# Leaving out two zeroings by GpSimd ahead of the first mixture-of-experts sums

## The chip, the cores and the metric

The kernel runs on one core of a Trainium2 chip. The metric is device time in microseconds (us) for one execution. The engines work side by side, each through its own queue in order: TensorE (PE; PEld are its weight loads), VectorE (DVE), ScalarE (ACT), GpSimd (POOL) and SyncE (SP), whose queue here issues most DMAs.

## The reference

Causal attention with a decay bias on (4, 8, 576, 64), then a top-1 mixture of 8 experts on the 2304 resulting rows of 512, then a feed-forward layer with h·cos(h):

```python
scores = scale * q @ k.T + minimum(-(cum_i - cum_j), 0)      # causal
attn   = softmax(scores);  x = (attn @ v) as (2304, 512)
idx    = argmax(xn @ en.T / tau);  gate = softmax(...)[idx]
for e in range(8):
    h = maximum(x[idx == e] @ w1[e], 0)
    out[idx == e] = gate * (h @ w2[e])
h = out @ w_in;  y = (h * cos(h)) @ w_out                    # 2304 x 512
```

## The kernel before, in words

Three stages follow each other, and their seams overlap. `attention` runs to about 215 us. It routes the rows batch by batch: POOL scatters each batch's rows to `xr` in DRAM, grouped by expert (L431). After the third of four batches one expert is chosen, and the first 256 of its rows are read back early and transposed into `the` and `tle`.

`moe1` is the first stage of sums. It takes nine "rounds": round -1 is the chosen expert on those 256 early rows, round 0 the same expert on its late 128 rows, rounds 1 to 7 the other experts. Each round has 8 steps f, one per slice of 128 hidden units. A step has a first product, `emit_h` (L727 to L729: 4 blocks, each as high·high, high·low and low·high halves, 12 matmuls), a relu that ACT writes as high half `hh` (L732) and DVE completes as low half `hl` (L733), and a second product `emit_o` one step later (L760 to L762: 12 matmuls into four sums `acc`). In TensorE's queue this gives h(n), o(n-1), h(n+1), o(n) and so on. At the end of a round the four sums go to SBUF: ACT writes the high half into `x2h` (L767), DVE the low half into `x2l` (L768), each at a column offset of that expert that is read from a register. `x2h` and `x2l` hold 2304 columns for all experts, and `moe2` reads them for the last two products.

Weights come through a ring of six slots. SP loads a chunk (L660) when a slot is free, ACT casts it to the high half (L662), DVE subtracts for the low half (L664). Round 0 uses full fp32 weights without a split: two chunks fill one slot (L657). SP's queue holds, in order: the eight chunks of round -1, three pairs for round 0, the late rows `xw` (L675), the first rows of round 1, the last pair of round 0, chunks of round 1. A load into a slot waits until the o step that last read it is done.

Beside this, DVE works through small operations of `counts` (L538 to L575), which sort the experts; ACT, DVE and SP read their results as registers (`pki`, L584 and L591).

The two zeroings stand in `moe1` before its loop, behind the last scatter of `attention` on POOL's queue. They set columns 344 to 2303 of `x2h` and `x2l` to zero, 4 x 1960 = 7840 fp32 a partition each. The sums written later cover the columns of the routed rows; a column that no round writes belongs to a row that the tail loop `overflow` computes again. SP's order is fixed by the program; DVE's, ACT's and POOL's order comes from a scheduler.

Of the kernel before, what the change touches and what calls it, by code (L numbers as in the profile page):

```python
# [7 lines left out]
F32 = mybir.dt.float32  # L8
# [10 lines left out]
B, H, S, D = 4, 8, 576, 64  # L19
NT, DM = 2304, 512  # L20
E, F = 8, 1024

EARLY, LATE = 256, 128
# [15 lines left out]
@with_exitstack  # L39
def moe_kernel(ctx, tc, qd, kd, vd, sd, ied, embt, tau, ident, maskd, trid, wcat, wf, out):  # L40
    nc = tc.nc
    const = ctx.enter_context(tc.tile_pool(name="const", bufs=1))
    dram = ctx.enter_context(tc.tile_pool(name="dram", bufs=1, space=DRAM))
    xr = dram.tile([E * NT, DM], F32, name="xr")
    count = ctx.enter_context(tc.tile_pool(name="count", bufs=1))

    g = G()
    g.count = count
    early = ExitStack()
    ep = early.enter_context(tc.tile_pool(name="early", bufs=1, side="right"))  # L50
    g.the = ep.tile([128, 4, EARLY], F32R, name="the")
    g.tle = ep.tile([128, 4, EARLY], F32R, name="tle")
    g.tc, g.nc, g.const, g.dram, g.xr, g.out = tc, nc, const, dram, xr, out
    with tc.manual_schedule(engines={mybir.EngineType.SP, mybir.EngineType.PE}):
        attention(g, qd, kd, vd, sd, ied, embt, tau, ident, maskd, trid)
    with tc.manual_schedule(engines={mybir.EngineType.SP}):
        st = ctx.enter_context(ExitStack())
        g.rawp = st.enter_context(tc.tile_pool(name="rawp", bufs=3, reuse_waits="tile"))
        g.ringp = st.enter_context(tc.tile_pool(name="ringp", bufs=RING, reuse_waits="tile"))
        g.x2p = st.enter_context(tc.tile_pool(name="x2p", bufs=1, reuse_waits="tile"))  # L60
        g.cv = st.enter_context(tc.tile_pool(name="cv", bufs=1, reuse_waits="tile"))
        g.chunks, g.tasks, g.loading = {}, [], {}
        moe1(g, wcat, wf)
        early.close()
        moe2(g, wf)
        st.close()
    with tc.manual_schedule():
        overflow(g, wcat, wf)
# [446 lines left out]
def moe1(g, wcat, wf):  # L515
    tc, nc, const, dram, xr = g.tc, g.nc, g.const, g.dram, g.xr
    SL = NT + CAPS[1]
    x2p = g.x2p
    x2h = x2p.tile([128, 4, SL], F32R, name="x2h")
    x2l = x2p.tile([128, 4, SL], F32R, name="x2l")  # L520
    g.x2h, g.x2l = x2h, x2l
    tid = g.tid = dram.tile([NT, 1], I32, name="tid")
    with ExitStack() as st:
# [118 lines left out]
            nc.vector.tensor_copy(out=g.win, in_=win)  # L642


        steps = [(r, f) for r in range(-1, E) for f in range(8)]
        loads = [(-1, f) for f in range(8)] + [(0, f) for f in range(0, 8, 2)] + [(r, f) for r in range(1, E) for f in range(8)]

# [137 lines left out]
                tc.declare_no_dep(ins.ins, o, reason="rows that differ")  # L785
            prev.append(ins.ins)


        c0 = (B - 1) * S // E + LATE
        with tc.issue_after(g.last.ins):  # L790
            nc.gpsimd.memset(x2h[:, :, c0:NT].bitcast(F32), 0.0)
            nc.gpsimd.memset(x2l[:, :, c0:NT].bitcast(F32), 0.0)
        NS = len(steps)
        for n in range(NS):
            r, f = steps[n]
# [289 lines left out]
```

## Time and profile before

| | |
|---|---|
| median of 3 runs (lowest, highest) | 893.03 us (891.38, 895.02) |
| the profiled execution | 895.34 us, of which the span is 893.5 us |
| mean granted TensorE clock | 0.982 |
| PE busy, DVE, ACT, POOL | 853.0, 612.4, 435.1, 139.2 us |
| `attention` / `moe1` / `moe2`, about | 0 to 215 / 215 to 480 / 480 to 893 us |

The span runs from the first to the last instruction; what lies around it is 1.8 us. Of TensorE's clock, 1.00 stands for 2.4 GHz and 0.50 for 1.2 GHz. In a timeline, an operation's time runs to its end, so operations of one engine that stand in its pipeline together overlap.

### The profile page before, as it was taken

What the parts mean: (1) busy time and instruction counts of PE and PEld (TensorE: products, weight loads), DVE (VectorE), ACT (ScalarE), POOL (GpSimd) and SP (SyncE); (2) the same over time, 40 slices, a digit from 0 to 9 for tenths busy, and PEclk for the clock granted to TensorE, in tenths of its full rate; (3) what the DMA queues carried; (4) which work ended last, traced back from release to release, by engine and by line L of the source; (5) the groups of instructions that cost most, each with busy time, mean ns of one, the idle gap of its engine ahead of it and who ended that gap; (6) DMA issues with size and microseconds to landing.
All of it is one profiled execution on the core that took longest, in us unless ns stands there. A gap on an engine that the chain in (4) does not pass through costs nothing. (4 is left out here: it accounts for less than half of the span.)

```text
span 893.5 us, 14901 instructions
## 1 busy us (share of the span) xinstructions
PE 853.0 (95%) x5286; PEld 691.0 (77%) x5286; DVE 612.4 (69%) x1611; ACT 435.1 (49%) x928; POOL 139.2 (16%) x156
## 2 busy tenths in 40 slices
PE   7999999997499999999999999999999999999994
PEld 3556565656499999999998888888888888888883
DVE  4778878887928555655679977777687748644452
ACT  3876767764325444554545555333343334333331
POOL 3422726340800111111000000000000000000132
PEclk9999999998799999999999999999999999999998
DMA  9999756313485676697654221111021100000112
GB/s 257 257 320 250 244 151 215 105 55 121 145 313 190 147 169 164 134 177 186 168 165 119 72 93 48 48 48 48 14 70 50 47 12 0 1 1 1 47 74 95
DMA packets 41871, 107.69 MB, mean 121 GB/s; under 512 B 9022, under 2 KB 9406, under 8 KB 41790
## 3 DMA queue, kind: packets, MB, share of 16 engines
q1 hardware_dynamic: 38190, 97.14, 38.6%
q0 software_dynamic: 3552, 9.45, 2.8%
q8 instruction: 44, 0.72, 0.3%
q14 instruction: 37, 0.30, 0.1%
q10 hardware_dynamic: 48, 0.07, 0.0%
HBM read 90.83 MB, written 15.81 MB: 119 GB/s over the span
## 5 line engine op out<-in xcount | busy, mean ns | idle before, releaser
L664 DVE TENSOR_TENSOR wl<-wraw,wh 128x1024 fp32r<-128x1024 f32 x64 | 78.4, 1226 | 75.3 <-ACT wh L662 72.5
L985 PE MATMUL h_ps<-x2h,wh 128*128 128x512 f32 (+1 forms) x320 | 118.3, 371 | 0.0
L987 PE MATMUL h_ps<-x2h,wl 128*128 128x512 f32 (+1 forms) x320 | 118.3, 370 | 0.0
L986 PE MATMUL h_ps<-x2l,wh 128*128 128x512 f32 (+1 forms) x320 | 118.1, 369 | 0.0
L1005 PE MATMUL facc<-wh,gh 128*128 128x512 f32 x288 | 114.8, 399 | 1.5 <-ACT gh L992 1.5
L1007 PE MATMUL facc<-wh,gl 128*128 128x512 f32 x288 | 113.9, 396 | 0.0
L1006 PE MATMUL facc<-wl,gh 128*128 128x512 f32 x288 | 113.8, 395 | 0.0
L846 ACT ACTIVATE ki<-h_ps 128x512 int32<-128x512 f32 (+1 forms) x80 | 44.6, 557 | 119.4 <-PE h_ps L987 114.4
L847 DVE SCALAR_TENSOR_TENSOR ki<-ki,h_ps 128x512 f32<-128x512 int32 (+1 forms) x80 | 50.6, 632 | 71.1 <-ACT ki L846 65.3
L662 ACT CAST wh<-wraw 128x1024 fp32r<-128x1024 f32 x64 | 67.0, 1048 | 61.2 <-PE acc L761 45.6
L283 ACT ACTIVATE s_sb<-s_sb,mx 128x576 f32<-128x576 f32 (+2 forms) x144 | 83.7, 583 | 21.1 <-DVE mx L278 17.4
L761 PE MATMUL acc<-hl,wh 128*128 128x256 f32 (+7 forms) x256 | 77.8, 305 | 12.8 <-DVE hl L733 12.8
L1017 POOL DMA_INDIRECT out_dram<-oacc,ti x18 | 17.5, 972 | 434.6 <-DVE oacc L1015 431.0
L848 ACT ACTIVATE ki<-ki,hpi 128x512 f32<-128x512 f32 (+1 forms) x80 | 54.5, 682 | 47.0 <-DVE ki L847 46.3
L762 PE MATMUL acc<-hh,wl 128*128 128x256 f32 (+7 forms) x256 | 77.4, 303 | 0.0
L760 PE MATMUL acc<-hh,wh 128*128 128x256 f32 (+7 forms) x256 | 76.6, 305 | 0.0
L992 ACT CAST gh<-ki 128x512 fp32r<-128x512 f32 (+1 forms) x80 | 46.2, 578 | 51.6 <-DVE ki L849 51.1
L986 PEld LDWEIGHTS h_ps<-x2l,wh 128*128 128x128 f32 x320 | 60.1, 188 | 12.3 <-issue 0.4
L985 PEld LDWEIGHTS h_ps<-x2h,wh 128*128 128x128 f32 x320 | 60.0, 188 | 12.2 <-issue 0.2
L987 PEld LDWEIGHTS h_ps<-x2h,wl 128*128 128x128 f32 x320 | 60.1, 188 | 11.2
L849 DVE TENSOR_TENSOR ki<-h_ps,ki 128x512 f32<-128x512 f32 (+1 forms) x80 | 50.7, 634 | 25.8 <-ACT ki L848 24.2
L727 PE MATMUL h_ps<-xth,wh 128*128 128x368 f32 (+6 forms) x224 | 68.2, 304 | 0.0
(218 smaller groups left out, 1884.4 us busy)
## 6 DMA issues: line engine op xcount, KB each, us to landing
wraw<-in_wcat_dram SPq DMA_DIRECT2D x64, 512.0 KB
wraw<-in_wf_dram SPq DMA_DIRECT2D x32, 512.0 KB
c_t<-cumd SPq DMA_DIRECT2D x15, 576.0 KB
xr<-zr SPq DMA_DIRECT2D x8, 768.0 KB
v_t<-in_vd_dram SPq DMA_DIRECT2D x16, 320.0 KB
q_t<-in_qd_dram SPq DMA_DIRECT2D x16, 288.0 KB
k_t<-in_kd_dram SPq DMA_DIRECT2D x16, 288.0 KB
c_t<-cumd SPq DMA_DIRECT2D x30, 144.0 KB
```

The source lines that it names most:

```text
L283: nc.scalar.activation(out=t[:, o:o + q1], in_=t[:, o:o + q1], func=ACTF.Exp, scale=-1.0, bias=mx, accum_out=rs[b][:, i, hd:hd + 1])
L664: nc.vector.tensor_tensor(out=lo, in0=raw, in1=hi.bitcast(F32), op=ALU.subtract)
L727: nc.tensor.matmul(out=ps[:, 0:c], lhsT=wh[:, sl], rhs=th[:, k, 0:c], start=(k == 0), stop=False)
L760: nc.tensor.matmul(out=ps[:, 0:c], lhsT=wh[:, sl], rhs=hh[:, 0:c], start=(f == 0), stop=False)
L761: nc.tensor.matmul(out=ps[:, 0:c], lhsT=wh[:, sl], rhs=hl[:, 0:c], start=False, stop=False)
L762: nc.tensor.matmul(out=ps[:, 0:c], lhsT=wl[:, sl], rhs=hh[:, 0:c], start=False, stop=(f == 7))
L985: nc.tensor.matmul(out=ps[:, 0:w], lhsT=wh[:, sl], rhs=g.x2h[:, k, a0:a1], start=(k == 0), stop=False)
L986: nc.tensor.matmul(out=ps[:, 0:w], lhsT=wh[:, sl], rhs=g.x2l[:, k, a0:a1], start=False, stop=False)
L987: nc.tensor.matmul(out=ps[:, 0:w], lhsT=wl[:, sl], rhs=g.x2h[:, k, a0:a1], start=False, stop=(k == 3))
L1005: nc.tensor.matmul(out=acc[t], lhsT=gh[:, sl], rhs=wh[:, 512:1024], start=(c == s), stop=False)
L1006: nc.tensor.matmul(out=acc[t], lhsT=gh[:, sl], rhs=wl[:, 512:1024], start=False, stop=False)
L1007: nc.tensor.matmul(out=acc[t], lhsT=gl[:, sl], rhs=wh[:, 512:1024], start=False, stop=(c == e))
```

## The change

Five lines with the two zeroings go; a blank line is added further up. So lines 645 to 787 of the kernel before are one higher after, and those from 794 on are four lower.

```diff
-        c0 = (B - 1) * S // E + LATE
-        with tc.issue_after(g.last.ins):
-            nc.gpsimd.memset(x2h[:, :, c0:NT].bitcast(F32), 0.0)
-            nc.gpsimd.memset(x2l[:, :, c0:NT].bitcast(F32), 0.0)
         NS = len(steps)
```

On POOL's queue, before, the zeroings stand between the last five scatters of routed rows and the scatters of token numbers (`tid`):

```order
L188 TENSOR_TENSOR rc<-ra,half_146 128x5
L431 DMA xr<-x,pi 18432x512 x5
L791 MEMSET x2h 128x4x1960
L792 MEMSET x2l 128x4x1960
L782 DMA tid<-tk,cpi 2304x1 x20
```

After:

```order
L188 TENSOR_TENSOR rc<-ra,half_146 128x5
L431 DMA xr<-x,pi 18432x512 x5
L783 DMA tid<-tk,cpi 2304x1 x20
L1013 DMA out_dram<-oacc,ti 2304x512 x18
```

Two rows left POOL's queue. The rows of the other engines are the same in the same order, apart from line and buffer numbers; one wait on POOL goes from the queue of ACT, at the first write of `x2h` at a register's offset (round 0). Before:

```order
L732 ACTIVATE hh<-h_ps 128x368 [waits PE_49,Activation_49]
L767 ISA
L767 COPY x2h<-acc_3714 128x128 [waits DVE_49,PE_49,Pool_49]
L767 ISA
L767 COPY x2h<-acc_3716 128x128 [waits DVE_49,PE_49]
```

After:

```order
L733 ACTIVATE hh<-h_ps 128x368 [waits PE_49,Activation_49]
L768 ISA
L768 COPY x2h<-acc_3712 128x128 [waits DVE_49,PE_49]
L768 ISA
L768 COPY x2h<-acc_3714 128x128 [waits DVE_49,PE_49]
```

Only the name `Pool_49` is gone from the first of these writes.

## Rows read from the trace of the kernel before

**Rows 1.** The page: busy time by engine, granted clock in 40 slices.

```profile
PE 853.0 (95%) x5286; PEld 691.0 (77%) x5286; DVE 612.4 (69%) x1611; ACT 435.1 (49%) x928; POOL 139.2 (16%) x156
...
PEclk9999999998799999999999999999999999999998
```

**Rows 2.** Waits of PE from 228 us on: total us, times, longest.

```profile
PE acc L761 <- DVE hl L733: 12.8, 2, 12.6
PE facc L1005 <- ACT gh L992: 1.5, 2, 1.3
PE h_ps L718 <- ACT x L696: 0.7, 1, 0.7
```

**Rows 3.** Timeline of PE: start, us, operation, count, idle before and releaser.

```profile
230.81 0.63 PE L760 MATMUL acc<-hh,wh 128*128 128x256 f32 x4
244.01 0.58 PE L761 MATMUL acc<-hl,wh 128*128 128x256 f32 x1 [12.56 <-DVE hl L733]
...
260.32 0.60 PE L695 MATMUL xt_ps<-idt,xw 128*128 128x128 f32 x4
...
274.62 1.06 PE L718 MATMUL h_ps<-x,w 128*128 128x128 f32 x8
```

**Rows 4.** Timeline of DVE, 223 to 245 us.

```profile
223.47 1.26 DVE L430 TENSOR_SCALAR x<-x,gt 128x512 f32<-128x512 f32 x3
...
225.45 0.16 DVE L562 CAST pki<-pick 128x8 int32<-128x8 f32 x1
...
226.75 0.42 DVE L733 SCALAR_TENSOR_TENSOR hl<-h_ps,hh 128x256 fp32r<-128x256 f32 x1
...
229.70 1.29 DVE L664 TENSOR_TENSOR wl<-wraw,wh 128x1024 fp32r<-128x1024 f32 x1 [0.97 <-ACT wh L662]
230.92 12.97 DVE L562 CAST pki<-pick 128x8 int32<-128x8 f32 x1
...
231.20 12.69 DVE L733 SCALAR_TENSOR_TENSOR hl<-h_ps,hh 128x256 fp32r<-128x256 f32 x1
243.94 0.22 DVE L561 TENSOR_REDUCE pick<-tmp 128x8 f32<-128x64 f32 x1
```

**Rows 5.** Timeline of POOL, 223 to 245 us.

```profile
223.99 1.26 POOL L431 DMA_INDIRECT xr<-x,pi  x1 [7.48 <-ACT x L428]
...
229.74 0.90 POOL L431 DMA_INDIRECT xr<-x,pi  x1 [0.30 <-issue]
230.62 6.66 POOL L791 MEMSET x2h<- 128x7840 f32 x1
237.20 6.66 POOL L792 MEMSET x2l<- 128x7840 f32 x1
```

**Rows 6.** Stretches, PE alone: length, PE busy (matmuls), clock, DMA share, GB/s.

```profile
225.86:231.44 5.58, 5.58 (x48) 1.00 0.92 289
244.01:249.72 5.71, 5.71 (x27) 0.50 0.45 149
```

**Rows 7.** Timeline of ACT: the casts of the last two weight chunks of round -1.

```profile
232.61 1.05 ACT L662 CAST wh<-wraw 128x1024 fp32r<-128x1024 f32 x1 [0.79 <-DMA wraw<-in_wcat_dram]
...
244.50 1.05 ACT L662 CAST wh<-wraw 128x1024 fp32r<-128x1024 f32 x1 [10.85 <-DVE pki L562]
```

**Rows 8.** Timeline of SP's DMA issues.

```profile
222.59 6.38 SPq L660 DMA_DIRECT2D wraw<-in_wcat_dram  x3
246.01 8.22 SPq L657 DMA_DIRECT2D w<-in_wcat_dram  x6
255.25 0.34 SPq L675 DMA_DIRECT2D xw<-xr  x1
```

**Rows 9.** Stretches: PE, PEld, DVE, ACT, POOL busy, clock, DMA share, GB/s.

```profile
234.00:236.00 2.00, 0.00 (x0) 0.00 (x0) 2.00 (x4) 0.00 (x0) 2.00 (x1) 1.00 0.03 12
246.00:260.00 14.00, 14.00 (x107) 14.00 (x107) 3.23 (x8) 2.09 (x6) 0.00 (x0) 0.87 0.81 286
255.00:260.00 5.00, 5.00 (x45) 5.00 (x44) 0.99 (x3) 1.17 (x4) 0.00 (x0) 1.00 1.00 368
```

## The prediction

> **What bounds the kernel now.** I read the busy shares first: TensorE is busy 853.0 of 893.5 us, far ahead of VectorE, and its granted clock is full in nearly all of the 40 slices, with a dip in the tenth and eleventh (223 to 268 us) [rows 1]. So a change on GpSimd, busy 16%, matters only if TensorE waits on something that GpSimd holds. The second view is TensorE's waits from 228 us to the end [rows 2]: 15 us in five waits, and one alone has 12.6 us. Everywhere else TensorE is the bound, so what this wait loses the end gets back, unless something else is late in its place. The timeline gives its place: the four matmuls L760 that begin at 230.81 are the last before the gap, and L761 starts at 244.01 after 12.56 us idle, released by `hl`, the low half of the relu, from VectorE [rows 3].
>
> The third view is VectorE's timeline there [rows 4]. Four operations, of which the rows show the first and the last, the cast L562 and the wanted L733, start between 230.92 and 231.20, and all show nearly 13 us: each ends at 243.89. The same cast took 0.16 us at 225.45, and the same L733 0.42 us at 226.75. They wait for nothing in the queue; they stand inside the engine. GpSimd's timeline has the partner [rows 5]: the zeroing of `x2h` begins at 230.62, that of `x2l` at 237.20, and they end at 237.28 and 243.86. VectorE was stuck from 0.3 us after the first began until 0.03 us after the second ended.
>
> The Trainium skill (SBUF — State Buffer, section "Who interferes with whom") says that VectorE and GpSimd share one pair of SBUF ports, that a copy or cast can take it, that a GpSimd operation holds it for the whole instruction, and that a two-input VectorE operation collides only with GpSimd's reads, not with one that only writes. The trace agrees that something blocks VectorE outright; whether only the cast at the head does, with the other three queued behind it, no row here can tell.
>
> **The change part by part.** Removed are 2 instructions of 6.66 us on GpSimd. By themselves they are free: nothing on GpSimd is late. What counts is what they hold.
>
> Term 1, the stall. Without the zeroings L733 still issues at 231.20 behind the three small operations, and takes 0.42 us: done at 231.62. Before, TensorE restarted 0.12 us after VectorE's release (243.89 to 244.01), so it now restarts at 231.74 [rows 3, 4]. Gain 244.01 - 231.74 = 12.27 us; about 0.3 us of waiting stays.
>
> Term 2, the clock after the stall. Between 244.01 and 249.72 the clock stood at 0.50, the 1.2 GHz level, and 27 matmuls took 5.71 us. Directly before the gap, at full clock, 48 matmuls of the same shape took 5.58 us, 0.116 us each [rows 6]. Without a long gap I expect no fall: 27 x 0.116 = 3.14 us in place of 5.71, gain 2.57 us. Bounds: if the clock fell all the same, 0; it can't give more than 2.57, since at 249.72 it was full again.
>
> Term 3, what is late next. Behind the stall stand three chains.
> - The last weight chunk of round -1. Its cast on ScalarE stood at 244.50 because ScalarE, in order, waited 10.85 us for a register value of the stuck cast L562 [rows 7]. That value is now there at 231.1, and the chunk's transfer decides. It was the last issue before 229 [rows 8], and in 234 to 236 us the DMAs are all but idle (share 0.03) [rows 9], so it lands about 234, at the latest 236. Cast 1.05, subtraction on VectorE 1.22 to 1.29 [rows 4, 7]: ready between 236.4 and 238.3. TensorE needs it for the eighth first product, 8 + 72 matmuls of 0.116 us after 231.74, at 241.0. But the `hl` of the fifth step stands behind that subtraction on VectorE, and TensorE wants it at about 237.3 (8 + 36 + 4 matmuls). That one waits between 0 and 1.4 us. I take 0, as the idle DMAs put the landing at the early end.
> - The loads of round 0. The first waits until the third second product is done: before, 2.0 us after the restart, 1.69 of them for eight slow matmuls, now 0.93 + 0.31 = 1.24 us after 231.74, at 233.0 against 246.01 [rows 8]. Ahead of the late rows `xw` lie 6 x 512 KB, with them 3.41 MB. TensorE needs `xw` at 260.32 - 14.84 = 245.5 [rows 3]. At 286 GB/s, the mean of 246 to 260 us, 3.41 MB takes 11.9 us and is there at 244.9; at 368 GB/s, 9.3 us [rows 9]. Scatters and the last chunk still move until about 234, which costs up to another 1.5 us: the wait is 0 to 0.9 us. I take 0.3 us, since the estimate and the need lie so close.
> - The rest of round 0. Until its last matrix 5.21 MB are queued; at 286 GB/s they are there at 251.2. TensorE's last first product of the round stands at 274.62, moved to 259.8 [rows 3]: 8.6 us to spare. From there on loads are tied to freed ring slots and move with TensorE. No cost.
>
> ScalarE's wait on GpSimd at the first `x2h` write of round 0 goes too; GpSimd was done at 243.86, long before round 0 could write its sums (its last first product starts at 274.62 [rows 3]), so it is worth 0.
>
> Sum: 12.27 + 2.57 - 0.3 = 14.5 us (1.6%). The profiled execution, 895.34 us, becomes 880.8, its span 879.0. It lies 2.3 us above the median of the runs shown (893.03); against that median I forecast 893.03 - 14.5 = 878.5 us.
>
> **The rivals.**
> - *The gain is partly given back.* The weights and rows behind the seam are late: both bounds of term 3 together, 2.3 us, or the clock falls once more, 2.57 us. For it speaks that `xw` has only some half a microsecond in hand, against it that the DMAs idle for ten microseconds in the stall and only move earlier. Gain about 12 us: 881.0.
> - *Only half of the stall belongs to the zeroings.* By the rule of the Trainium skill just named (whoever comes first holds the ports for one whole instruction) the cast that had waited since 230.92 should have got the ports when the first zeroing ended; then the rest would have another cause. As a mechanism of this kernel: VectorE stays held by something else for the 6.6 us from 237.28 to 243.89. TensorE restarts 6.6 us later than forecast, the gain is 5.7 us and the clock still falls: 887.4. Against it: the release comes 0.03 us after the second zeroing ends, the second starts 0.08 us before the first ends, and the scatters, the only other work of GpSimd in reach, did not hold VectorE: the TENSOR_SCALARs at 223.47 ran 1.26 us for three while a scatter stood from 223.99 to 225.25 [rows 4, 5].
> - *The change does nothing.* VectorE's hold ends with the zeroings by coincidence: 893.0. One coincidence of 0.03 us in 13 speaks against it.
> - *Slower.* The round 0 loads now follow directly on the scatters and chunks of the seam; if they ran at a far lower rate than in 246 to 260 us, TensorE would stand for them at its last first product of round 0. The 5.21 MB from 233.0 must be there by 259.8, that is 194 GB/s; all of the gain is lost at 5.21 MB in 41.3 us, 126 GB/s, and 0.5% beyond it at 114 GB/s. Then 897.5 us. Against it: 286 and 368 GB/s with the same queue in use, and 289 GB/s with the scatters beside it [rows 6, 9].
>
> **How the numbers follow.** The forecast gets 0.83, the partial return 0.07, half 0.05, nothing 0.03, slower 0.02. About 0.5%, 4.5 us, is what a measurement of this kernel can tell from no change; forecast, partial return and half (-0.63%) lie beyond it on the fast side: faster 0.95, same 0.03, slower 0.02. Range: the best gain, 14.84 us, under a median lower by the spread of the runs (1.7 us), 876.5, and a little less; at the other end the partial return with the spread upward (2.0 us), 883.0, and a little more towards the half: 876.0 to 884.0.
>
> **What would show it.** Right: L734 (L733 before) lasts about 0.4 us at 231 us, TensorE has no wait over 1.5 us between 228 us and the end, its clock stays at 1.00 from 226 us on, the last matmul ends 14 to 15 us earlier, and attention up to 230 us is unchanged. Wrong: VectorE operations of several microseconds remain behind 231 us; a wait of TensorE on `xw` or on a weight of round 0 over 2 us; a stretch at 0.50 behind 232 us.

## The result and the profile after

Without the zeroings the kernel takes 881.92 us (median of 4 runs, 879.86 to 882.89) against 893.12 us (4 runs): ratio 0.987 (95% interval 0.984 to 0.990). Two more comparisons on other chips, told below, give 0.984 (0.982 to 0.986) and 0.986 (0.984 to 0.988). By the three ratios the gain is 11.5, 14.2 and 12.6 us. One execution of the changed kernel, of 1186.63 us at a granted clock of 0.657, was slow as a whole and is left out of every figure here. The profiled execution takes 881.11 us, its span is 879.3 us. Lines between 645 and 787 of before are one higher here.

The page, against [rows 1], busy time by engine and granted clock in 40 slices:

```profile
PE 852.3 (97%) x5286; PEld 689.4 (78%) x5286; DVE 600.0 (68%) x1611; ACT 435.0 (49%) x928; POOL 126.4 (14%) x154
...
PEclk9999999999899999999999999999999999999998
```

TensorE does the same work in the same busy time; its share rises because the span shrinks. VectorE's busy time falls by 12.4 us without losing an instruction: that was time inside the stuck operations. The waits of TensorE from 226 us to the end, against [rows 2] (each line: total us, times, longest):

```profile
PE xt_ps L696 <- DMA xw<-xr: 0.8, 1, 0.8
PE h_ps L719 <- ACT x L697: 0.7, 1, 0.7
PE acc L762 <- DVE hl L734: 0.3, 1, 0.3
```

The 12.6 us are gone; a new wait of 0.8 us on the late rows `xw` has come. The 0.3 us for `hl` lie behind 400 us, where the profile of before has them too. VectorE, where [rows 4] had four operations of nearly 13 us, and TensorE's restart, where [rows 3] had 244.01:

```profile
232.18 0.16 DVE L562 CAST pki<-pick 128x8 int32<-128x8 f32 x1
232.25 0.22 DVE L560 TENSOR_TENSOR tmp<-sel,cnt 128x64 f32<-128x64 f32 x1
232.39 0.16 DVE L566 TENSOR_TENSOR dl<-off,eb 128x8 f32<-128x8 f32 x1
232.47 0.42 DVE L734 SCALAR_TENSOR_TENSOR hl<-h_ps,hh 128x256 fp32r<-128x256 f32 x1
```

```profile
232.29 0.64 PE L761 MATMUL acc<-hh,wh 128*128 128x256 f32 x4
232.94 0.39 PE L762 MATMUL acc<-hl,wh 128*128 128x256 f32 x1
...
247.97 0.66 PE L696 MATMUL xt_ps<-idt,xw 128*128 128x128 f32 x4 [0.78 <-DMA xw<-xr]
```

The same four operations take 0.16 to 0.42 us each, and the matmul that waited for `hl` starts 0.05 us after it, 0.01 us after the four in front of it. Behind it the granted clock stays at 1.00 (2.4 GHz), against 27 matmuls at 0.50 in [rows 6] (PE alone: length, busy, clock, DMA share, GB/s):

```profile
232.94:246.90 13.96, 13.96 (x115) 1.00 0.93 339
```

SP's issues, against [rows 8], come earlier, by each profile's own time: the loads of round 0 by 11.8 us, the late rows `xw` by 13.3 us:

```profile
234.18 6.74 SPq L658 DMA_DIRECT2D w<-in_wcat_dram  x6
241.94 0.34 SPq L676 DMA_DIRECT2D xw<-xr  x1
```

The time scales of two executions differ by what happened before the seam: the first matmul of round -1 (L727) starts at 217.25 us before and at 218.94 us after, in a stage that the change doesn't touch. So I compare from that matmul on, before and after:

```profile
217.25 0.56 PE L727 MATMUL h_ps<-the,wh 128*128 128x256 f32 x1
```

```profile
218.94 0.56 PE L728 MATMUL h_ps<-the,wh 128*128 128x256 f32 x1
```

To the transposes of `xw` (L695 before, L696 after) it is 43.07 us before and 29.03 us after: 14.0 us gained in the seam. 1.7 us of it are hidden by the later start; on the other side `moe2` has in this execution none of the 1.5 us of waiting at L1005 that the one before had. That makes some 13.8 of the 14.2 us between the two spans; the other 0.4 us I have not placed.

### The profile page after: what moved, and what is told of

Same layout as the page of the kernel before. It is cut to its first block, busy times and chain, and to the rows that moved or that the text cites. A ratio compares the mean times of both kernels' runs of the same rounds, so it can differ in the third digit from the quotient of the medians.

```text
span 879.3 us, 14899 instructions
## 1 busy us (share of the span) xinstructions
PE 852.3 (97%) x5286; PEld 689.4 (78%) x5286; DVE 600.0 (68%) x1611; ACT 435.0 (49%) x928; POOL 126.4 (14%) x154
## 5 line engine op out<-in xcount | busy, mean ns | idle before, releaser
L982 PEld LDWEIGHTS h_ps<-x2l,wh 128*128 128x128 f32 x320 | 60.1, 188 | 12.4 <-DVE x2l L769 0.8
L981 PEld LDWEIGHTS h_ps<-x2h,wh 128*128 128x128 f32 x320 | 60.0, 188 | 12.2
L728 PE MATMUL h_ps<-xth,wh 128*128 128x368 f32 (+6 forms) x224 | 68.2, 304 | 0.0
```

The source lines that it names most:

```text
L728: nc.tensor.matmul(out=ps[:, 0:c], lhsT=wh[:, sl], rhs=th[:, k, 0:c], start=(k == 0), stop=False)
L981: nc.tensor.matmul(out=ps[:, 0:w], lhsT=wh[:, sl], rhs=g.x2h[:, k, a0:a1], start=(k == 0), stop=False)
L982: nc.tensor.matmul(out=ps[:, 0:w], lhsT=wh[:, sl], rhs=g.x2l[:, k, a0:a1], start=False, stop=False)
```

## The experiments

**The gain measured again.** The changed kernel without an edit, in five rounds, and again beside the second set of experiments.

> The changed kernel once more, in five rounds. The sum read from the profiles (14.5 us) gives a ratio to before of 0.984; the medians so far (893.12 and 881.92 us) give 0.987. If the sum holds, the ratio is 0.983 to 0.986; if a part of the sum was a feature of the one profiled execution of before (its 895.34 us is the slowest known), it stays at 0.986 to 0.989, a gain of 10 to 12.5 us. In the profile: no VectorE operation over 2 us behind 231 us, TensorE waits 0.3 us on hl and up to 1 us on xw in both cases.

> The changed kernel beside the three others on the same chip, to compare them with: ratio to before 0.983 to 0.986, as the sum of 14.5 us and the last run say.

Ratios 0.984 (0.982 to 0.986) and 0.986 (0.984 to 0.988): both lie where the sum put them, the first comparison (0.987) did not. In each profile the seam lasts as in the first one: 28.97 and 28.89 us from the first matmul of round -1 to the transposes of `xw`. So the seam of the changed kernel hardly varies, and I looked for the looser part in the kernel before (below). Outside the seam the changed kernel varies too: its three profiled executions take 879.21 to 885.74 us.

**One zeroing in place of two.** The line with `x2l` goes:

```diff
             nc.gpsimd.memset(x2h[:, :, c0:NT].bitcast(F32), 0.0)
-            nc.gpsimd.memset(x2l[:, :, c0:NT].bitcast(F32), 0.0)
```

> Only the zeroing of x2h is left in, that of x2l goes. Theory (VectorE is held exactly as long as a zeroing runs): the hold ends with the one zeroing, 6.7 us after its start, TensorE's wait on hl falls from 12.6 to about 5.9 us, and 6.6 us are gained, plus 0 to 2.6 us of clock: 884 to 886.5 us where before has 893. Rival (only a part of the hold belongs to the zeroings, the end of it has another cause): the wait stays longer than 7 us, 887 to 893 us.

Ratio 0.992 (0.990 to 0.994): 7.0 us gained, half of what both give on this chip. VectorE and GpSimd in its profile:

```profile
229.72 0.16 DVE L562 CAST pki<-pick 128x8 int32<-128x8 f32 x1
...
230.70 6.56 DVE L562 CAST pki<-pick 128x8 int32<-128x8 f32 x1
231.84 5.42 DVE L733 SCALAR_TENSOR_TENSOR hl<-h_ps,hh 128x256 fp32r<-128x256 f32 x1
```

```profile
230.57 6.66 POOL L791 MEMSET x2h<- 128x7840 f32 x1
```

The hold ends at 237.26, 0.03 us after the one zeroing. So its length is the zeroings' own, and the rival of another cause for its second half falls. One thing was not expected: the cast at 229.72 slipped through ahead of the zeroing, and the next cast, 0.13 us behind the zeroing's start, was held. TensorE therefore got one second product and one first product further before it stood, and waits 4.1 us where 5.9 us were expected.

**The zeroings kept, the casts written another way.**

```diff
-                nc.vector.tensor_copy(out=pki[n], in_=pick[:, n, :])
+                nc.vector.tensor_tensor(out=pki[n], in0=pick[:, n, :], in1=pick[:, n, :], op=ALU.max)
```

> Both zeroings stay; the three small VectorE casts L562 (128x8, fp32 to int32) are written as tensor_tensor max of the row with itself, so VectorE runs no copy, cast or tensor_scalar while the zeroings run. Theory A (only the one-input cast at the head collides with a GpSimd operation that only writes; the other three stood behind it): no VectorE operation over 2 us, TensorE's wait on hl 0.3 to 0.5 us, time as with the zeroings left out, 879 to 883 us. Theory B (any VectorE operation on SBUF is held by a running zeroing): the tensor_tensor shows nearly 13 us in its place, TensorE waits 12.6 us, 892 to 894 us.

882.47 us, beside 882.0 us for the changed kernel on the same chip (the median of its six executions that count); ratio to before 0.986 (0.984 to 0.989). In the seam TensorE waits 0.3 us for `hl`. GpSimd and VectorE:

```profile
230.19 6.67 POOL L791 MEMSET x2h<- 128x7840 f32 x1
236.81 6.65 POOL L792 MEMSET x2l<- 128x7840 f32 x1
```

```profile
230.69 0.16 DVE L562 TENSOR_TENSOR pki<-pick 128x8 int32<-128x8 f32 x1
230.77 0.22 DVE L560 TENSOR_TENSOR tmp<-sel,cnt 128x64 f32<-128x64 f32 x1
230.90 0.16 DVE L566 TENSOR_TENSOR dl<-off,eb 128x8 f32<-128x8 f32 x1
230.98 0.41 DVE L733 SCALAR_TENSOR_TENSOR hl<-h_ps,hh 128x256 fp32r<-128x256 f32 x1
231.31 0.21 DVE L561 TENSOR_REDUCE pick<-tmp 128x8 f32<-128x64 f32 x1
```

Both zeroings run their full 13.3 us, and VectorE works beside them at its usual speed. Theory A holds: of all that stood in [rows 4], only the cast of 8 elements a partition collided; the other three were queued behind it. Within the noise the whole gain is to be had with the zeroings left in. The Trainium skill (SBUF — State Buffer, section "Who interferes with whom") says that a copy or cast can take the ports that GpSimd uses, and that an operation with two inputs in SBUF meets GpSimd's reads and not a GpSimd operation that only writes. The trace agrees, with 0.16 us for the two-input form against 12.97 us for the cast, on the same 8 elements a partition.

**The zeroings in eight pieces.** The two zeroings are replaced by these lines, once high and low in turn, once the four of `x2h` first:

```diff
+            for d in range(4):
+                nc.gpsimd.memset(x2h[:, d, c0:NT].bitcast(F32), 0.0)
+                nc.gpsimd.memset(x2l[:, d, c0:NT].bitcast(F32), 0.0)
```

```diff
+            for t in (x2h, x2l):
+                for d in range(4):
+                    nc.gpsimd.memset(t[:, d, c0:NT].bitcast(F32), 0.0)
```

> The two zeroings are written as eight of 1960 elements a partition, some 1.7 us each, high and low in turn, the same 13.3 us in all. Theory A (the ports are held for one instruction and whoever waits gets them next): VectorE is held for at most one piece, TensorE's wait on hl is 0.3 to 2 us, 879 to 884 us. Theory B (queued GpSimd instructions follow each other without letting VectorE in, as the second zeroing of before started 0.08 us before the first ended): VectorE is held to the end of the last piece, wait 12 to 13 us, 892 to 894 us.

> Eight pieces of zeroing again, but the four of x2h first, which wait for no DMA and so follow each other directly for 6.7 us behind the last scatter. Theory A (a waiting VectorE operation gets the ports when one GpSimd instruction ends): the cast is held for at most one piece, 1.8 us, TensorE's wait on hl is under 2 us, ratio to before 0.983 to 0.988. Theory B (GpSimd's next queued instruction starts before the one in front has ended, and keeps VectorE out): the cast is held for all four pieces, some 6.5 us, TensorE waits about 6 us, ratio 0.990 to 0.994.

In turn: ratio 0.985 (0.983 to 0.988), all of the gain. `x2h` first: 0.9995 (0.998 to 1.001), none. The first of the two, GpSimd and then VectorE:

```profile
230.59 1.76 POOL L792 MEMSET x2h<- 128x1960 f32 x1
235.68 1.74 POOL L793 MEMSET x2l<- 128x1960 f32 x1 [3.33 <-DMA xr<-x,pi]
```

```profile
231.11 1.27 DVE L562 CAST pki<-pick 128x8 int32<-128x8 f32 x1
...
231.40 0.99 DVE L733 SCALAR_TENSOR_TENSOR hl<-h_ps,hh 128x256 fp32r<-128x256 f32 x1
```

and the second:

```profile
230.31 6.76 POOL L793 MEMSET x2h<- 128x1960 f32 x4
237.00 6.76 POOL L793 MEMSET x2l<- 128x1960 f32 x4
```

```profile
230.92 12.88 DVE L562 CAST pki<-pick 128x8 int32<-128x8 f32 x1
```

The first order doesn't test what I meant it to test: the first piece of `x2l` had to wait 3.33 us for the scatters, and VectorE got in during that pause, at 232.38. In the second order GpSimd has no pause, and eight pieces hold the cast as long as two long zeroings: 12.88 us, of which TensorE waits 12.2 us. That is theory B, though longer than its numbers (about 6 us of waiting, ratio 0.990 to 0.994): the pieces of `x2l` had nothing left to wait for at 237.00, so all eight follow each other. So in these two profiles a waiting cast gets in where GpSimd pauses, not where one instruction ends and the next follows. The section of the Trainium skill just named says that the ports are held for the whole instruction; here a run of eight instructions kept the cast out.

**The clock alone.** The kernel before, with 48 filler matmuls in the stall (an excerpt: one more line each names `g.hl` and keeps the matmul behind the fillers in its place):

```diff
+            if n == 2:
+                wp = ps_t.tile([128, 512], F32, tag="t", name="w_ps")
+                with tc.issue_after(g.hl.ins):
+                    for _ in range(48):
+                        nc.tensor.matmul(out=wp, lhsT=g.ones_b, rhs=g.ones_b.unsqueeze(1).to_broadcast([128, 4, 128]), start=True, stop=True)
```

> The kernel before with both zeroings, and 48 filler matmuls (bf16, 512 columns, 10.3 us at full clock, into a spare PSUM bank) between the fourth first product and the third second product of round -1, where TensorE stands for 12.6 us. The stall stays, TensorE only isn't idle in it. If term 2 of the prediction is right: the clock stays at 1.00 up to and behind the restart, the wait on hl falls to some 2 us, and the kernel is 2.6 us faster than before, ratio 0.996 to 0.998. Rival (the clock after the stall costs nothing on the path, since a transfer or the register loads are due then): ratio 0.999 to 1.002.

Ratio 0.9955 (0.994 to 0.997), 2.4 to 5.6 us faster than before, though the cast is held as long as ever (13.14 us). Its timeline of TensorE, and the stretch behind the release:

```profile
220.18 0.56 PE L727 MATMUL h_ps<-the,wh 128*128 128x256 f32 x1
...
232.98 10.53 PE L756 MATMUL w_ps<-ones_b 128*128 128x512 bf16 x48
...
247.21 0.38 PE L766 MATMUL acc<-hl,wh 128*128 128x256 f32 x1 [0.74 <-DVE wl L664]
...
258.22 0.66 PE L695 MATMUL xt_ps<-idt,xw 128*128 128x128 f32 x4
```

```profile
247.00:253.00 6.00, 5.79 (x49) 1.00 0.85 315
```

The clock stays at 1.00. The profile gives the gain more closely. In it too the first cast slipped through, as in three profiles of the kernel before further down; the seam, from L727 to L695, takes 38.04 us here and 40.05, 41.22 and 40.26 us there, so 2.0 to 3.2 us are gained in it. Term 2 is real, and its 2.57 us lie in the middle. What the rest of the 4.0 us (893.87 us at 0.9955) is stays open; the fillers also move the third second product behind themselves, and the ScalarE relu of the fourth step moves in its queue, which the experiment does not separate.

**The clock at the start of the seam.** The changed kernel, with fillers in the 3.4 us wait ahead of L395:

```diff
             if b == B - 1:
                 early_rows()
+                wp = ps_s.tile([128, 512], F32, tag="s", name="w_ps")
+                for _ in range(14):
+                    nc.tensor.matmul(out=wp, lhsT=ones_b, rhs=ones_b.unsqueeze(1).to_broadcast([128, 4, 128]), start=True, stop=True)
```

> The changed kernel (no zeroings) with 14 filler matmuls (bf16, 512 columns, 3.0 us at full clock) in the 3.4 us in which TensorE waits for the last routing, ahead of L395. In the profile of the changed kernel the clock stands at 0.50 from 216.9 to 227.1 us, behind that wait. If the wait brings the fall and the fillers prevent it, the 10.2 us there shrink to 6 to 9 us and the kernel is 1 to 4 us faster than the changed one, ratio to before 0.980 to 0.983; if the fall has been set by the idle spells before 213 us already, or VectorE's weight subtractions are the bound there, the ratio stays at 0.984; if the fillers delay L395, 0.985 to 0.988.

Ratio 0.986 (0.984 to 0.988), the same as the changed kernel beside it. TensorE with the fillers, and then without:

```profile
220.00:223.40 3.40, 3.40 (x16) 0.50 0.59 188
223.40:231.00 7.60, 7.39 (x62) 1.00 0.88 308
```

```profile
220.00:225.80 5.80, 5.80 (x28) 0.50 0.73 262
225.80:231.00 5.20, 5.20 (x46) 1.00 0.89 294
```

The stretch at 0.50 became 3.4 us long, shorter than expected, but the gain that was tied to that did not come: the transposes of `xw` start 29.05 us after the first matmul of round -1 with the fillers and 28.89 us without. The seam's first weights and the late rows are waited for in both: 2.2 us for a weight of the first step and 0.7 us for `xw` with the fillers, 1.7 and 0.6 us without. I found no version faster than the changed kernel.

**The kernel before, profiled again.** Three more executions of the kernel before, unedited, to see why the medians gain less than the first profile promised.

> One more profile of the kernel before. In the profile on which the prediction rests, the first of the two casts L562 behind 229 us started 0.3 us behind the first zeroing and was held. In the two experiments with a zeroing at the same place whose profiles show it otherwise (one zeroing, fillers), that cast slipped through ahead of the zeroing and the next one, some 1 us later, was held. Theory: both happen in executions of the kernel before too; where the first slips through, TensorE still does the third second product and the fifth first product (24 matmuls, 2.8 us at most), its wait is 9.5 to 11 us in place of 12.6, and the execution is 1.5 to 3 us shorter, 890 to 893 us against 894 to 897. Rival: the hold always begins with the first cast, the wait is 12 to 13 us in each profile, and the spread of the runs has another place.

> As for the look before it: either the first cast is held and TensorE waits 12 to 13 us, or it slips through and TensorE waits 9.5 to 11 us in an execution that is 1.5 to 3 us shorter.

> As for the two looks before it: 12 to 13 us of waiting with the first cast held, or 9.5 to 11 us with the first cast through and 1.5 to 3 us less time; if all three looks show 12 to 13 us, the spread of the runs of before is not from here.

In all three the first cast slips through. VectorE, GpSimd and TensorE in the first of them:

```profile
233.13 0.16 DVE L562 CAST pki<-pick 128x8 int32<-128x8 f32 x1
...
233.41 0.41 DVE L733 SCALAR_TENSOR_TENSOR hl<-h_ps,hh 128x256 fp32r<-128x256 f32 x1
...
234.11 13.13 DVE L562 CAST pki<-pick 128x8 int32<-128x8 f32 x1
...
236.62 10.63 DVE L664 TENSOR_TENSOR wl<-wraw,wh 128x1024 fp32r<-128x1024 f32 x1
```

```profile
233.98 6.66 POOL L791 MEMSET x2h<- 128x7840 f32 x1
240.56 6.65 POOL L792 MEMSET x2l<- 128x7840 f32 x1
```

```profile
247.32 0.58 PE L761 MATMUL acc<-hl,wh 128*128 128x256 f32 x1 [10.71 <-DVE wl L664]
```

The first cast is through 0.85 us ahead of the zeroing, the wanted `hl` with it; the next cast is held for 13.13 us, but TensorE does a second product and a first product more before it stands, for 10.7 us.

| execution | first cast | wait | at 0.50 behind it | L727 to L695 (after: L728 to L696) | time |
|---|---|---|---|---|---|
| before, the profile of the prediction | held | 12.6 | 5.7 | 43.07 | 895.34 |
| before, three more | through | 10.7, 10.7, 10.7 | 3.8, 5.0, 3.9 | 40.05, 41.22, 40.26 | 893.80, 891.73, 894.39 |
| eight pieces, `x2h` first | held | 12.2 | 2.8 | 41.65 | 892.39 |
| changed, three profiles | no zeroing | 0.0, 0.4, 0.0 | none | 29.03, 28.97, 28.89 | 881.11, 885.74, 879.21 |

All times are in us. The fourth column is read from TensorE's stretches behind the wait, here of the three more and of the eight pieces:

```profile
247.32:251.09 3.77, 3.77 (x17) 0.50 0.05 16
244.66:249.61 4.95, 4.95 (x23) 0.50 0.24 75
247.22:251.14 3.92, 3.92 (x18) 0.50 0.16 20
243.92:246.76 2.84, 2.84 (x13) 0.50 0.00 0
```

The seam's gain is 14.0 us against the profile of the prediction and 11.0 to 12.3 us against the three more. So both terms of the stall vary from one execution to the next: the wait with the cast that meets the zeroing, and the length of the stretch at 0.50 behind it, 2.8 to 5.7 us. The expected 890 to 893 us of the short way failed for the first and third of the three: their first matmul of round -1 started at 220.25 and 220.34 us, not at 217, three microseconds that arise before the seam. What sets those three microseconds, and the length of the low stretch, I have not tried.

## Why the prediction was right, point by point

- *The bound and the culprit.* Right: one wait, made by the zeroings through VectorE. The cast experiment shows the mechanism and the single zeroing its length.
- *Term 1, 12.27 us.* Right for the execution on which it rested: where 0.3 us of waiting was to stay, TensorE stands 0.01 us (0.4 and 0.0 us in the two other profiles). Too large for the kernel: four profiles of before show a wait of 12.6 us once and 10.7 us three times. Which cast meets the zeroing is a race of less than a microsecond (0.30 us behind it in [rows 4, 5], 0.85 us ahead in the first of the three more), and I read one outcome as the only one. That can explain a gain below 14.5 us, but not more than that: which way the executions without a profile went is not on record, and the start of the seam shifts by 3 us as well.
- *Term 2, 2.57 us.* The fall of the clock was on the path, and it's gone. The fillers give 2.4 to 5.6 us by the times and 2.0 to 3.2 us by the seam. Its size, too, belonged to one execution: a stretch at 0.50 of 5.7 us, where other profiles have 2.8 to 5.0 us.
- *Term 3, 0.3 us.* The right place, too small: `xw` came 0.78 us late, within the bound of 0.9. The wait of the fifth step's `hl`, bounded by 0 to 1.4 us and taken as 0, is below what the table of waits shows. Weights of round 0 cost nothing, as forecast. Their first load was issued 1.24 us after the restart (232.94 to 234.18), as forecast, though the eight slow matmuls taken as 1.69 us lasted 1.88 us (244.01 to 245.89 in TensorE's timeline).
- *Partial return* (clock or transfers) took no more than 0.5 us of the seam in the first pair of profiles. *Half* fell with the single zeroing, *nothing* with the result. The step by which *half* was reached, that a waiting cast gets in when one zeroing ends, is what the eight pieces contradict. *Slower*: DMA ran at 339 GB/s from 232.94 to 246.90 us, where these loads lie, not under the 126 GB/s from which all would have been lost.
- *The number.* 881.92 us lies in the range (876.0 to 884.0), 3.4 us above the forecast. I had taken the sum from the slowest execution of before then known (895.34 us) and set it against the median; a sum read from such an execution should have been shortened, not only shifted. That 881.92 us lies within the range is no proof of each term's size.
- *The signs.* `hl` lasts 0.42 us, no wait behind 228 us is over 0.8 us, and the last matmul starts 14.3 us earlier (882.20 to 867.89). Two hold only with the 1.7 us taken off by which the seam starts later: the clock is at 1.00 from 227.1 us on, not from 226, and attention is not at the same time as before. The dip of the clock in the tenth and eleventh slice of [rows 1] is 201 to 246 us, not 223 to 268; nothing else was taken from it.

## What to carry to other kernels

A long fill by GpSimd is not free because GpSimd is idle: look on VectorE's timeline for a group of operations that end together just behind a GpSimd instruction, with a short copy or cast at its head; the others may only be queued behind it. The remedy may be smaller than leaving the fill out: write the cast as a two-input operation. Splitting the fill helped only where a pause of GpSimd stood between the pieces. Where a stall begins with a race, read several executions before its length goes into a sum.

## What the runs showed of the hardware that was not expected

- Eight fills of 1.7 us in a row by GpSimd held one VectorE cast of 8 elements for 12.88 us, about as long as two fills of 6.66 us did (12.97 us). Where a pause of 3.33 us followed the first fill, the cast was done 0.03 us after that fill ended.
- Beside a fill by GpSimd (with the cast written as a two-input operation), tensor_tensor, scalar_tensor_tensor and tensor_reduce of VectorE ran at their usual 0.16 to 0.41 us.
- The clock level of 0.50 cost 2.0 to 3.2 us behind the stall. At the start of the seam, shortening a stretch at 0.50 from about 10 to 3.4 us gained nothing that the times or the seam show; weights and rows were waited for there with and without.
